# Attention chunks of 128 tokens split into two halves of 64, and the attention of a pair of chunks spread over three places between the weight products

## The chip, the cores and the metric

The kernel runs on one core of one Trainium2 chip. The metric is the device time of one execution in microseconds (us). Before the change it is 352.75 us, the median of 9 runs (352.5 to 353.03). A core has TensorE (called PE in the profile, with PEld for its weight loads), VectorE (DVE), ScalarE (ACT), GpSimd (POOL), and SyncE (SP), whose queue issues nearly all transfers here.

## The reference, cut to what matters

First comes a linear attention with decay, over 4 batches, 8 heads, 768 tokens and a head size of 48; then a feed-forward block on the 3072 tokens with d_model 384 and d_ff 1024.

```python
for t in range(S):
    cur = np.einsum('bhd,bhe->bhde', u[None] * kt, vt)
    y[:, :, t] = np.einsum('bhd,bhde->bhe', rt, state + cur)
    state = w[None, :, :, None] * state + np.einsum('bhd,bhe->bhde', kt, vt)
...
h = x @ w_in
e = np.exp(h - h_max)
solu = h * (e / (np.sum(e, axis=-1, keepdims=True) + 1e-09))
ln = (solu - mu) / np.sqrt(var + 1e-06) * g_ln
out = ln @ w_out
```

Everything is float32.

## The kernel before, in words

The tokens are cut into N = 24 chunks of T = 128 tokens, ordered so that the four batches alternate: chunk i belongs to batch i mod 4 and is its chunk number i // 4. Each batch has a state in SBUF, 128 partitions by 4 head pairs: the two heads of a pair lie in partitions 0-47 and 64-111.

The steps of one chunk, each a small function inside `direct_path`:

- `decay_k`, `decay_r`, `weigh` (L666 to L683, POOL): k and r times powers of the decay, and r·k·u per element; `sum_own` (L685, DVE) sums that per head, and `diagonal` (L689, ACT) writes it onto the diagonal of AT, the transposed score matrix, with eight instructions of 128 by 128 (L693).
- r and k are turned so that the head size lies on partitions. For the first nine chunks TensorE does it (`turn_r` L701, evicted by DVE; `turn_k` L708, evicted by ACT), from chunk 9 on a transposing DMA (`halve_rk` L872, `join_rk` L882).
- `scores` (L721): for each head pair a, half c and head q one product of 48 rows by 64 columns, with 128 moving columns for the first half of the keys and 64 for the second. `take_scores` (L732, DVE) copies them into AT under a mask, two instructions of 128 by 512.
- `heads` (L750): y, transposed, in tiles of 128 rows by 32 columns with 128 moving columns: 12 products of the state with r (not for the first chunk of a batch) and 16 of v with AT. `take_y` (L774, ACT) evicts it as xT.
- `outer` (L779): k times v in tiles of 128 by 32 with 48 moving columns; `update` (L794) adds it to the state on DVE and multiplies by the decay on POOL.
- `ffn_in` (L809): xT times w_in into h_ps, a buffer of two PSUM banks that exists once, then the exponential on ACT. `unit` (L820): a reciprocal and h times e on DVE (L826, the last reader of h_ps), then two ACT passes. `halve_ln`, `join_ln` (L861, L867): the result is turned by a transposing DMA between an ACT copy and a DVE copy. `ffn_out` (L886): the product with w_out, an ACT eviction, the store.

A float32 product appears in the trace as two matmul instructions, each with its own weight load; so a chunk's `scores` are 32 instructions, `heads` 56, `outer` 32, `ffn_in` 12 and `ffn_out` 16.

The order is written out by hand, engine by engine; each engine executes its instructions in that order. A first loop (L906, i = -2 to 6) runs one chunk per pass: from i = 2 on `ffn_in(i-2)`, the turns of chunk i+2, scores of i+1, `heads(i)`, `outer(i)`, while DVE, ACT and POOL also convert the float64 weights. The main loop (L998, i = 7, 9, ... 29) runs two chunks per pass: `ffn_in(i-2)`, `ffn_out(i-7)`, `ffn_in(i-1)`, `ffn_out(i-6)`, and then all the attention of the pair at once: scores of i+1 and i+2, `heads` of i and i+1, `outer` of both. The eight PSUM banks are two for h_ps, four fixed banks `pss` for scores and turns, and two in rotation (tag "m") for y_ps, kv_ps and o_ps.

## Time and profile before

| | |
|---|---|
| median of 9 runs | 352.75 us |
| the profiled execution's own time | 352.62 us |
| its span in the profile | 350.9 us |
| granted TensorE clock | 0.999 |
| PE busy | 334.3 us, 95%, 3427 matmuls |
| ACT, DVE, POOL busy | 240.3, 210.7, 178.8 us |
| chain that ended last, on PE | 79% |

The profile is one execution. Its time is 1.72 us longer than its span, which is the time around the recorded instructions. "PE busy" counts a matmul from its start to a modelled end, and matmuls overlap; how long a group takes is better read from the start of its first instruction to the start of the next group's first. A line such as `x32 | 26.3, 279 | 0.0` has the number of instructions, their busy time in us, the mean duration of one in ns, and the idle time before them. "128*32 128x128" is a tile of 128 rows by 32 columns of the array, with 128 rows by 128 moving columns streamed through it.

### The profile page before, as it was taken

What the parts mean: (1) busy time and instruction counts of PE and PEld (TensorE: products, weight loads), DVE (VectorE), ACT (ScalarE), POOL (GpSimd) and SP (SyncE); (2) the same over time, 40 slices, a digit from 0 to 9 for tenths busy, and PEclk for the clock granted to TensorE, in tenths of its full rate; (3) what the DMA queues carried; (4) which work ended last, traced back from release to release, by engine and by line L of the source; (5) the groups of instructions that cost most, each with busy time, mean ns of one, the idle gap of its engine ahead of it and who ended that gap; (6) DMA issues with size and microseconds to landing.
All of it is one profiled execution on the core that took longest, in us unless ns stands there. A gap on an engine that the chain in (4) does not pass through costs nothing.

```text
span 350.9 us, 8480 instructions
## 1 busy us (share of the span) xinstructions
PE 334.3 (95%) x3427; PEld 204.8 (58%) x3427; DVE 210.7 (60%) x347; ACT 240.3 (68%) x457; POOL 178.8 (51%) x196
## 2 busy tenths in 40 slices
PE   2699999999999999999999999999999999999993
PEld 2485566655664665575575575475575575555563
DVE  7795888896577568378368468469466162323420
ACT  3765988988868966866866866866867755546510
POOL 3889667789259439539539629629624000000000
PEclk9999999999999999999999999999999999999999
DMA  8999987269999999987999878865993523553541
GB/s 169 266 234 226 235 187 131 46 104 195 188 187 151 217 195 133 200 147 133 175 162 150 202 129 152 202 134 103 144 164 70 129 67 64 126 127 101 134 103 35
DMA packets 164878, 52.76 MB, mean 150 GB/s; under 512 B 157917, under 2 KB 161245, under 8 KB 164829
## 3 DMA queue, kind: packets, MB, share of 16 engines
q1 hardware_dynamic: 164684, 51.92, 78.6%
q8 instruction: 29, 0.48, 0.6%
q10 hardware_dynamic: 144, 0.20, 0.3%
q14 instruction: 21, 0.16, 0.2%
HBM read 26.94 MB, written 4.72 MB: 90 GB/s over the span
## 4 chain that ended last, share of the span: by engine, by line
PE 79%; ACT 7%; DVE 5%; issue 3%; DMA 2%; POOL 2%; POOLq 0%; DVEq 0%; ACTq 0%
PE o_ps L896 34%; PE h_ps L814 30%; PE y_ps L761 8%; PE at L728 5%; ACT AT L693 2%; ACT halves L864 2%; DVE solu L826 1%; DMA halves<-halves 1%; PE kv_ps L791 1%; DVE part L532 1%; ACT e L817 1%; DMA wq<-in_w_dram 1%; DVE AT L735 1%; ACT solu L828 1%; ACT e L829 1%
## 5 line engine op out<-in xcount | busy, mean ns | idle before, releaser
L814 PE MATMUL h_ps<-w_in_sb,xT 128*128 128x512 f32 x288 | 129.0, 597 | 1.2 <-DVE solu L826 0.7
L896 PE MATMUL o_ps<-w_out_sb,lnT 128*128 128x384 f32 (+1 forms) x400 | 127.5, 474 | 0.1
L896 PEld LDWEIGHTS o_ps<-w_out_sb,lnT 128*128 128x128 f32 x400 | 74.9, 190 | 53.1 <-issue 8.1
L814 PEld LDWEIGHTS h_ps<-w_in_sb,xT 128*128 128x128 f32 x288 | 53.5, 190 | 62.9 <-issue 57.4
L804 POOL TENSOR_TENSOR state<-state,pw 64x192 f32<-64x192 f32 x32 | 27.5, 860 | 69.2 <-DVE state L803 67.5
L693 ACT ACTIVATE AT<-ident,own 128x128 f32<-128x128 f32 x192 | 58.6, 391 | 4.9 <-DVE own L687 4.9
L864 ACT COPY halves<-solu 128x2048 uint16<-128x2048 uint16 x24 | 45.4, 1891 | 3.0 <-DMA halves<-halves 3.0
L669 POOL TENSOR_TENSOR kp<-kpad,kdec 128x512 f32<-128x512 f32 x24 | 41.5, 1729 | 6.9 <-ACT kdec L623 6.3
L828 ACT ACTIVATE solu<-solu,st 128x1024 f32<-128x1024 f32 x24 | 27.5, 1147 | 24.3 <-DVE solu L826 24.3
L817 ACT ACTIVATE e<-h_ps 128x1024 f32<-128x1024 f32 x24 | 24.5, 1019 | 25.5 <-PE h_ps L814 25.5
L735 DVE COPY_PREDICATED AT<-later,at 128x512 f32<-128x512 uint32 x48 | 31.6, 731 | 15.2 <-PE at L728 15.2
L858 DVE COPY lnT<-halves 128x2048 uint16<-128x2048 uint16 x24 | 33.6, 1419 | 6.7 <-DMA halves<-halves 6.5
L824 DVE RECIPROCAL st<-sums 128x1 f32<-128x1 f32 x24 | 3.9, 163 | 54.4 <-ACT e L817 54.2
L835 POOL TENSOR_SCALAR st<-st 128x1 f32<-128x1 f32 x24 | 7.3, 305 | 49.3 <-ACT e L829 49.2
L826 DVE SCALAR_TENSOR_TENSOR solu<-h_ps,st,e 128x1024 f32<-128x1024 f32 x24 | 30.8, 1284 | 2.1
L858 DVE COPY rk<-halves 128x2048 uint16<-128x2048 uint16 x15 | 29.3, 1953 | 0.0
L777 ACT COPY xT<-y_ps 128x384 f32<-128x384 f32 x24 | 11.5, 479 | 22.4 <-PE y_ps L761 22.4
L683 POOL TENSOR_TENSOR rku<-rku,rpad 128x384 f32<-128x384 f32 x23 | 25.7, 1115 | 1.8
L761 PE MATMUL y_ps<-AT,vt 128*32 128x128 f32 x768 | 26.3, 279 | 0.0
L898 ACT ACTIVATE o<-o_ps,st 128x384 f32<-128x384 f32 (+1 forms) x25 | 13.8, 554 | 18.1 <-PE o_ps L896 11.3
L728 PE MATMUL at<-rk 48*64 48x128 f32 (+1 forms) x768 | 26.2, 265 | 0.0
L829 ACT ACTIVATE e<-solu 128x1024 f32<-128x1024 f32 x24 | 25.4, 1057 | 0.8
(83 smaller groups left out, 346.0 us busy)
## 6 DMA issues: line engine op xcount, KB each, us to landing
raw<-in_moe_w_in_dram SPq DMA_DIRECT2D x12, 512.0 KB, 4.9
raw<-in_moe_w_out_dram SPq DMA_DIRECT2D x16, 384.0 KB, 3.9
kpad<-in_k_dram SPq DMA_DIRECT2D x24, 192.0 KB, 5.1
rpad<-in_r_dram SPq DMA_DIRECT2D x24, 192.0 KB, 5.4
vt<-in_v_dram SPq DMA_DIRECT2D x24, 192.0 KB, 5.1
out_dram<-o SPq DMA_DIRECT2D x23, 192.0 KB, 2.9
halves<-halves SPq DMA_TRANSPOSE x39, 4.9
u_bc<-in_u_dram ACTq DMA_DIRECT2D x1, 192.0 KB, 3.4
```

The source lines that it names most:

```text
L669: nc.gpsimd.tensor_mul(X["kp"].rearrange("p h d -> p (h d)"), kpads[i % NLD].rearrange("p h d -> p (h d)"), kdec.rearrange("p a d -> p (a ...
L693: nc.scalar.activation(out=AT[:, h, :], in_=ident, func=ACT.Copy, scale=X["own"][:, h])
L728: nc.tensor.matmul(ps[q][ts(c, P), a, c * P :], X["kT"][rows, a, ts(c, P)], X["rT"][rows, a, c * P :], start=True, stop=True)
L735: nc.vector.copy_predicated(A4[:, :, q, :], later.to_broadcast([128, HP, T]), live[i]["scores"][q])
L761: nc.tensor.matmul(y_ps[32 * g : 32 * g + 32, j, :], lhsT, rhs, start=(g not in opened), stop=stop, skip_group_check=True)
L814: nc.tensor.matmul(h_ps[:, ts(n, NX)], X["xT"][:, j, :], w_in_sb[:, j, ts(n, NX)], start=(j == 0), stop=(j == KD - 1))
L826: nc.vector.scalar_tensor_tensor(out=solu, in0=X["h"], scalar=rs, in1=X["e"], op0=ALU.mult, op1=ALU.mult, accum_out=tot)
L828: nc.scalar.activation(out=solu, in_=solu, func=ACT.Identity, scale=-float(dff), bias=tot)
L829: nc.scalar.activation(out=X["e"], in_=solu, func=ACT.Square, accum_out=ss)
L858: nc.vector.tensor_copy(out=words.bitcast(U16).rearrange("p n (t o) -> p o n t", o=2), in_=turned)
L864: nc.scalar.copy(out=both.rearrange("p (o n) -> p o n", o=2), in_=split(X["solu"]))
L896: nc.tensor.matmul(o_ps, X["lnT"][:, f, :], w_out_sb[:, f, part], start=(f == 0), stop=(f == KF - 1))
```

## The change

Each chunk from the third on is treated as two halves of 64 tokens, with a state between them.

- `scores` computes only the two 64 by 64 blocks on the diagonal (64 moving columns each); AT is 64 wide, `diagonal` writes 64 columns and `take_scores` moves 256 instead of 512 per head group.
- `outer` computes k times v for each half by itself, in tiles of 64 by 64, into two buffers. `middle` (new) makes the state between the halves, `mid`, from the first; `update` adds the second to `mid`. The last chunk of a batch needs only the first.
- y has two PSUM banks, one for each half. `within` (new): v times AT, each half by itself, in tiles of 64 rows by 32 columns with 64 moving columns. `carried` (new): the state times r for the first half, `mid` times r for the second, 64 moving columns each. `take_y` evicts with two instructions.
- In the main loop the work of a pair lies in three places: `attend` (scores, `outer`, `take_scores`, `middle` of the next pair) at the end of a pass, `within` after the first `ffn_in`, `carried`, `take_y` and `update` after the first `ffn_out`. The loads of k and r, POOL's decays, the turns and the diagonals are one chunk earlier; the first pass (`late`) therefore does three chunks of POOL's work and three turns instead of two.
- In the first loop `outer` and `middle` come right after `ffn_in`, both turns come before the weight conversions and `unit`, and turns and y share the two rotating banks "m". kv has two banks of its own; the scores' and, from chunk 7 on, y's banks are the same two. Chunks 0 and 1 are done as before.

```diff
+    def scores(chunks):
...
+            for a in range(HP):
+                for c in range(2):
+                    for q in range(2):
+                        nc.tensor.matmul(X["scores"][q][ts(c, U), a, :], X["kT"][rows, a, ts(c, U)],
+                                         X["rT"][rows, a, ts(c, U)], start=True, stop=True)
...
+    def within(chunks):
...
+            for n, (m, h, at) in enumerate(inner):
+                for c in range(2):
+                    nc.tensor.matmul(X["y"][c][ts(g, 32), j, :], vf[ts(c, U), at : at + 32],
+                                     AT[ts(c, U), h, :], start=(g not in opened), stop=closes,
+                                     skip_group_check=True)
...
+    def carried(i):
+        for c, St in enumerate((states[units[i][0]], X["mid"])):
+            if c == 0 and units[i][1] == 0:
+                continue
+            for m in range(12):
+                nc.tensor.matmul(X["y"][c][ts(g, 32), j, :],
+                                 St[:, a].rearrange("p q d -> p (q d)")[:, ts(n, 32)],
+                                 X["rT"][:, a, ts(c, U)], start=False, stop=True,
+                                 skip_group_check=True)
...
     def outer(chunks):
-            for a in range(HP):
-                for g in range(4):
-                    nc.tensor.matmul(X["kv"][ts(g, 32), a], X["kp"][:, h, ts(g % 2, 32)],
-                                     vt[:, h, 0:D], start=True, stop=True)
+            for a in range(HP):
+                for q in range(2):
+                    for c, dst in enumerate(X["kv"]):
+                        nc.tensor.matmul(dst[ts(q, P), a], X["kp"][ts(c, U), h, :],
+                                         vt[ts(c, U), h, 0:D], start=True, stop=True)
...
+    def middle(i):
+        for q in range(2):
+            to, kv = X["mid"][ts(q, P), :, q], X["kv"][0][ts(q, P)]
+            if c > 0:
+                nc.vector.tensor_add(to, kv, St[ts(q, P), :, q])
+            else:
+                nc.scalar.copy(out=to, in_=kv)
...
+    def attend(chunks):
+        scores(chunks)
+        outer(chunks)
+        for i in chunks:
+            take_scores(i)
+        for i in chunks:
+            middle(i)
...
+    attend([LA + LO, LA + LO + 1])
     for i in range(LA + LO, N + LA + LO, 2):
...
             ffn_in(j)
             unit(j)
+            within([i, i + 1])
...
         ffn_out(l)
+        for n in (i, i + 1):
+            if n < N:
+                carried(n)
...
         ffn_out(l + 1)
...
-        for n in now:
-            scores(n)
-        for n in now:
-            take_scores(n)
-        for n in now if i < N - 1 else []:
-            heads(n)
-            take_y(n)
-        outer(now)
+        attend([i + 2, i + 3])
```

## The prediction

> **What bounds the kernel now.** I read the page first, then PE's waits, then PE's timeline for one pass of the main loop, then the groups with shapes kept apart. The page says that TensorE is busy 95% of the span and solid from the third slice on; the two weight products alone take 129.0 and 127.5 us.

> ```profile
> PE 334.3 (95%) x3427; PEld 204.8 (58%) x3427; DVE 210.7 (60%) x347; ACT 240.3 (68%) x457; POOL 178.8 (51%) x196
> ...
> PE   2699999999999999999999999999999999999993
> ...
> L814 PE MATMUL h_ps<-w_in_sb,xT 128*128 128x512 f32 x288 | 129.0, 597 | 1.2 <-DVE solu L826 0.7
> L896 PE MATMUL o_ps<-w_out_sb,lnT 128*128 128x384 f32 (+1 forms) x400 | 127.5, 474 | 0.1
> ```

> PE's waits add to some 11 us, nearly all of them before 37 us; after that there are 0.17 us on L826 at 110.45 and 0.50 us of "issue" at 127.1. So from 36.41 us to the last o_ps, time changes by what PE has to do, and by new waits. One pass by the timeline:

> ```profile
> 174.89 1.96 PE L728 MATMUL at<-rk 48*64 48x128 f32 x64
> 176.79 0.86 PE L761 MATMUL y_ps<-rk,state 128*32 128x128 f32 x24
> 177.47 1.06 PE L761 MATMUL y_ps<-AT,vt 128*32 128x128 f32 x32
> 178.34 0.84 PE L761 MATMUL y_ps<-rk,state 128*32 128x128 f32 x24
> 179.00 1.06 PE L761 MATMUL y_ps<-AT,vt 128*32 128x128 f32 x32
> 179.87 0.86 PE L791 MATMUL kv_ps<-vt,kp 128*32 128x48 f32 x64
> 180.66 5.42 PE L814 MATMUL h_ps<-w_in_sb,xT 128*128 128x512 f32 x12
> 185.92 5.32 PE L896 MATMUL o_ps<-w_out_sb,lnT 128*128 128x384 f32 x16
> 191.08 5.31 PE L814 MATMUL h_ps<-w_in_sb,xT 128*128 128x512 f32 x12
> ```

> Starts to starts: `ffn_in` 5.16 (5.26 after kv), `ffn_out` 5.16, and the attention of the pair from 174.89 to 180.66. A pass is 180.66 - 154.08 = 26.58 us (the same line one pass earlier starts at 154.08); four undisturbed weight products are 20.62, so attention with its transitions costs **5.96 us**.

> **What one matmul costs.** The 32 of v with AT take 178.34 - 177.47 = 0.87 us. They go round four column tiles, 8 to a tile: 109 ns for 128 moving columns. kv takes 0.79 us for 64 here and 0.45 for 32 in the first loop (44.52 to 44.97); the difference, 0.34 for 32, gives 42.5 ns for 48 columns. A line through both: 0.83 ns a column plus 2.6. So 64 columns are **56 ns** in their tile. The scores agree: 16 matmuls of 128 columns follow each other in a first-half tile, 16 x 109 = 1.74 of the 1.90 us measured, and the 64-column tiles hide beside them. Sums: 1.74 + 28 x 109 ns (y) 3.05 + 16 x 42.5 ns (kv) 0.68 = 5.47; the remaining **0.49 us are transitions** between shapes. They can be placed: o to scores 0.09 (`ffn_out` from 185.92 to 191.08 takes 5.16, the one before the scores, 169.64 to 174.89, 5.25), scores to y 0.16, kv to h 0.11, h after kv 0.10, and 0.03 in y.

> ```profile
> L761 PE MATMUL y_ps<-AT,vt 128*32 128x128 f32 x768 | 26.3, 279 | 0.0
> L728 PE MATMUL at<-rk 48*64 48x128 f32 x384 | 26.2, 286 | 0.0
> L728 PE MATMUL at<-rk 48*64 48x64 f32 x384 | 21.2, 245 | 0.0
> L791 PE MATMUL kv_ps<-vt,kp 128*32 128x48 f32 x640 | 9.9, 209 | 0.5 <-issue 0.5
> ```

> **The change on PE, for a pair.**
> - Scores: still 64, all of 64 columns, over four tiles: 16 x 56 = 0.90 (before 1.74).
> - v with AT: 128 instead of 64, over eight tiles (two row halves by four columns): 16 x 56 = 0.90 (1.74). No row shows eight tiles. Bounds: 7.0 ns a matmul, if all eight run together, and 10.6 ns, the fastest pace that a group of the trace keeps (kv, 0.34/32); that end costs 0.46 more a pair. I take 7.0: kv's 10.6 is just its tile time divided by four tiles, so nothing else limits it, and the scores show that two row tiles run together.
> - State with r: 96 of 64 columns over four tiles: 24 x 56 = 1.34 (1.31).
> - kv: still 64, now 64 by 64. The weight loads bound it from above: means of 112, 139 and 190 ns (L791, L728, L896) for 32, 64 and 128 columns, about 0.8 ns a column, so 52 ns against 42.5 of streaming. Between 42.5 and 58 ns a matmul I take 52: 0.83 (0.68).
> - Transitions: three groups instead of one. Into a group 0.09, out of it 0.21, and 0.03 to 0.16 between scores and kv: 3 x 0.30 + 0.1 = about 1.0 (0.49).

> After: 0.90 + 0.90 + 1.34 + 0.83 + 1.0 = 4.97, so about **1.0 us saved a pair**. Over chunks 7 to 23: scores 17 x 0.42, v with AT 17 x 0.42, state -0.3, transitions -4.4, kv -1.0 and -0.8 for the half products that chunks 20 to 23 now need and did not have: **gain 7.8 us**.

> **The first loop, chunks 2 to 6.** There PE saves the same matmul time, but kv now stands alone behind `ffn_in` (two more transitions) and `within` and `carried` differ in shape: some 0.45 us more. For chunks 4 to 6 a pass of 9.25 us (44.97 to 54.22) becomes 8.95: 0.3 saved. Chunks 2 and 3 had no state product and now have half of one (0.34): nothing saved. Against that stand new waits. y takes the two banks that the turns just used, so `within` waits for DVE's rT (0.69 us, behind two `middle` adds of 0.35) and ACT's kT (0.57 us, behind the exponential of 1.2). For chunks 2 and 3 ACT also makes `mid`, two copies that I put at 0.33 each (L777: 0.48 for twice the columns): some 0.2 and 0.4 us lost, 0.1 for chunk 4.

> ACT is the second thing to watch; its timeline shows it late by itself in the last passes:

> ```profile
> 67.28 2.45 ACT L693 ACTIVATE AT<-ident,own 128x128 f32<-128x128 f32 x8
> 69.63 1.00 ACT L817 ACTIVATE e<-h_ps 128x1024 f32<-128x1024 f32 x1
> ...
> 78.11 2.44 ACT L693 ACTIVATE AT<-ident,own 128x128 f32<-128x128 f32 x8
> 80.46 1.00 ACT L817 ACTIVATE e<-h_ps 128x1024 f32<-128x1024 f32 x1
> ```

> `ffn_in` ended at 68.72 and its exponential began at 69.63, when the diagonals were done. This cost nothing: no one waited. Narrower diagonals save about 0.4 a chunk (306 ns start to start to some 255, by 0.75 ns a column from L898's two forms), a second y eviction gives 0.2 back, and the later rT delays L826 by some 0.6, so ACT stays as late as it was. But now (a) `within(6)` waits for kT, behind that exponential: about 1.5 us; (b) `within(8)` stands right behind `ffn_in(5)` and needs `take_scores(8)`, which needs the diagonal that ended at 80.46: about 0.9 us. What queues behind (b) on DVE is four `middle` adds, `sum_own(9)` and L826, until about 85; `ffn_in(6)` comes after `ffn_out(0)`, at about 88, so nobody waits for it. Sum for the first loop and its exit: 0.9 - 0.2 - 0.4 - 0.1 - 1.5 - 0.9 = **-2.2 us**; bounds +0.9 (every wait covered) and -4.5 (twice the waits).

> **The other engines in the main loop.** DVE loses 4 x 0.3 in `take_scores` and gains 4 x 0.36 in `middle`: nothing. `within` needs `take_scores` of the pair 7 us after the scores. `ffn_in(j)` must wait for L826 of the chunk before: `ffn_out` and attend, 7 us, against exponential, reciprocal and L826, 3 us. Cover gone, each would cost PE its full delay. POOL's decays no longer stand behind the state's multiplication of the same pair; its 16 us a pass fit into 25.6. The k and r loads go out a chunk earlier into five buffers that the decays have left; the extra POOL set, turn and join of the first pass have until attend at about 97 us, and I end them at 95. A stall there of 1 to 2 us is inside the range.

> **Sum.** 7.8 - 2.2 = 5.6 less: span 345.3, time 352.62 - 5.6 = 347.0. The profiled execution is 0.13 under the median, so this stands for the median too.

> [...]

> **Rivals.**
> 1. *Eight tiles don't all run together*, pace 10.6 ns: 17 chunks x 64 x 3.6 ns = 3.9 less gain, **350.9**. For it: no row shows eight tiles. Against: kv is explained by its tiles.
> 2. *The entry costs nothing*: ACT is early enough, gain 7.8 + 0.9 = 8.7, **343.9**. For it: shorter diagonals. Against: the exponentials of 69.63 and 80.46 are already late.
> 3. *Slower: row tiles pay a floor.* The only row-tiled group, L728, has 1.90 us for 64 = 29.7 ns a matmul. If that is a floor and not the 128-column tiles, the 256 row-tiled matmuls of a pair take 7.6 us; with 1.34 and 1.0 that is 9.9 against 5.96, +4.0 a pair, some 8 pairs: **about 385**. It decides from (5.96 - 1.34 - 1.0) / 256 = 14 ns on. Against: 16 x 109 ns explains the 1.90 without a floor.
> 4. *It does not save what it says*: transitions cost double in the new places (h to `within`, o to `carried`), 1 us more a pair: gain gone, **about 352**. Against: the four measured edges all lie at 0.09 to 0.21.

> **Chances.** Forecast 0.50 (345 to 349), rival 1 0.15, rival 2 0.15, rival 3 0.08, rival 4 0.12 (half of it slower, a third within 0.2%, the rest a little faster). 0.2% is about what a measurement of this kernel can tell from no change. From the same cases: faster 0.82, same 0.04, slower 0.14. The range takes in rivals 1 and 2 with the bounds of kv: 343.0 to 351.2.

> **What will show it.** Groups of the new profile: scores from 1.90 to about 1.05 a pair, `within` about 0.95 to 1.1, `carried` 1.4, kv 0.8 to 0.95; a pass of 25.6 us. PE's waits should show kT or DVE's `take_scores` between 60 and 83 us, 2 to 3 us in all, and none later. Wrong it would be with a new wait in every pass, or with `within` over 1.8 us a pair.

## The result, and the profile after

The changed kernel takes **362.0 us** in the median of 10 runs (355.2 to 364.6) against 352.75 (31 runs, 351.6 to 354.0): slower, ratio 1.0135, 95% interval 1.0104 to 1.0166. (The ratio leaves out runs more than 1.5% above the fastest, so it is below that of the medians; the profiled execution is such a run, and how much of its pauses the fastest, 355.2, had is not shown.) I had forecast 347.0 with 0.82 for faster: wrong, and the mechanism was in none of the rivals. The profiled execution took 360.84 us, 8.2 more than the 352.62 of before.

The page of the changed kernel, its lines in the order of those shown of before, and the instruction queue's:

```profile
PE 336.3 (94%) x4723; PEld 198.8 (55%) x4723; DVE 205.5 (57%) x387; ACT 234.7 (65%) x485; POOL 163.6 (46%) x203
...
PE   3688969997999999999999999999999999999993
...
PEclk9998998999999999999999999999999999999998
...
q8 instruction: 39, 0.64, 0.8%
...
L905 PE MATMUL h_ps<-w_in_sb,xT 128*128 128x512 f32 x288 | 133.2, 613 | 0.0
L987 PE MATMUL o_ps<-w_out_sb,lnT 128*128 128x384 f32 (+1 forms) x400 | 128.2, 476 | 0.0
```

TensorE is still the bound, but in the third, fourth, sixth and tenth slices there are holes where before had only nines from the third on, and the granted clock dips in the fourth and the seventh. The input products, the same 288 matmuls, now cost 133.2 us instead of 129.0. And the instruction queue moved 39 packets, where before had 29.

The main loop, which the prediction worked out in most detail, by TensorE's timeline (start, length):

```profile
162.40 1.16 PE L763 MATMUL at<-rk 48*64 48x64 f32 x64
163.38 1.10 PE L861 MATMUL kv_ps<-vt,kp 64*64 64x48 f32 x64
164.41 5.42 PE L905 MATMUL h_ps<-w_in_sb,xT 128*128 128x512 f32 x12
169.76 1.48 PE L822 MATMUL at<-AT,vt 64*32 64x64 f32 x128
171.17 5.43 PE L987 MATMUL o_ps<-w_out_sb,lnT 128*128 128x384 f32 x16
176.53 0.54 PE L835 MATMUL at<-rk,state 128*32 128x64 f32 x24
176.89 0.52 PE L835 MATMUL at<-rk,mid 128*32 128x64 f32 x24
177.22 0.52 PE L835 MATMUL at<-rk,state 128*32 128x64 f32 x24
177.56 0.52 PE L835 MATMUL at<-rk,mid 128*32 128x64 f32 x24
178.00 5.42 PE L905 MATMUL h_ps<-w_in_sb,xT 128*128 128x512 f32 x12
```

Start to start: scores 0.98, kv 1.03, v times AT 1.41, state times r 1.47. The same line one pass earlier starts at 138.30, so a pass is 164.41 - 138.30 = 26.11 us: 0.47 less than the 26.58 of before, not 1.0 less. From `ffn_in(7)` to the last output product it is 241.27 against 245.54 us, a **gain of 4.3**. But `ffn_in(7)` starts at 112.10 instead of 99.70: **the entry loses 12.4**, and 12.4 - 4.3 is the 8.1 us to be explained. TensorE's waits (all idle time, by line and what ended it):

```profile
PE y_ps L835 <- issue: 2.8, 1, 2.8
...
PE kv_ps L861 <- DVE state L896: 2.2, 1, 2.2
PE rd_ps L630 <- DVE state L894: 2.1, 1, 2.1
...
PE y_ps L822 <- DVE rk L724: 0.5, 1, 0.5
```

These four are 7.66 us. Two products behind them are slow; TensorE's timeline for the first of the four shows one:

```profile
48.15 0.42 PE L835 MATMUL y_ps<-rk,mid 128*32 128x64 f32 x15
51.40 0.33 PE L835 MATMUL y_ps<-rk,mid 128*32 128x64 f32 x9 [2.83 <-issue]
51.66 7.11 PE L905 MATMUL h_ps<-w_in_sb,xT 128*128 128x512 f32 x12
```

7.11 us (and 7.01 behind the pause of `rd_ps`) where 5.42 is the rule: 3.3 more. The trace's clock records show half clock for 3.41 us there. Pauses and half clock together are 11.0 of the 12.4. The other 1.4 is mostly not a loss: by `ffn_in(7)` the changed kernel has also done scores of chunk 10 and k times v of chunks 9 and 10, about 1.5 us by the times above, which before does behind `ffn_in(7)`. Counted by equal work the entry loses some 10.9 us and the main loop gains some 2.8. The passes of the first loop are longer too (62.66 to 72.19, 9.53 us, where before had 9.25), by some 1.1 us in all, about as much as the 1.2 us of waits that before has from 26 us to there (0.54, 0.48 and 0.17) and the changed kernel has not.

### The profile page after: what moved, and what is told of

Its sections match the earlier page's. It is cut to its first block, busy times and chain, and to the rows that moved or that the text cites. A ratio compares the mean times of both kernels' runs of the same rounds, so it can differ in the third digit from the quotient of the medians.

```text
span 359.1 us, 11106 instructions
## 1 busy us (share of the span) xinstructions
PE 336.3 (94%) x4723; PEld 198.8 (55%) x4723; DVE 205.5 (57%) x387; ACT 234.7 (65%) x485; POOL 163.6 (46%) x203
## 4 chain that ended last, share of the span: by engine, by line
PE 90%; DVE 3%; issue 3%; POOL 2%; ACT 0%; POOLq 0%; DVEq 0%
PE h_ps L905 37%; PE o_ps L987 35%; PE at L835 4%; PE at L822 3%; PE kv_ps L861 3%; PE at L763 3%; PE y_ps L822 1%; PE tk_ps L731 1%; PE y_ps L835 1%; PE tr_ps L723 1%; POOL kp L682 1%; PE at L746 1%; PE y_ps L794 1%; POOL vt L586 0%; DVE rk L724 0%
## 5 line engine op out<-in xcount | busy, mean ns | idle before, releaser
L905 PE MATMUL h_ps<-w_in_sb,xT 128*128 128x512 f32 x288 | 133.2, 613 | 0.0
L905 PEld LDWEIGHTS h_ps<-w_in_sb,xT 128*128 128x128 f32 x288 | 54.0, 194 | 61.6 <-issue 59.4
L897 POOL TENSOR_TENSOR state<-state,pw 64x192 f32<-64x192 f32 x36 | 18.3, 508 | 62.1 <-DVE state L896 60.3
L919 ACT ACTIVATE solu<-solu,st 128x1024 f32<-128x1024 f32 x24 | 27.5, 1147 | 27.9 <-DVE solu L917 27.7
L711 ACT ACTIVATE AT<-same,own 128x64 f32<-128x64 f32 x176 | 44.4, 338 | 1.4 <-DVE own L700 1.4
L949 DVE COPY lnT<-halves 128x2048 uint16<-128x2048 uint16 x24 | 38.9, 1637 | 5.9 <-DMA halves<-halves 5.7
L695 POOL TENSOR_TENSOR rku<-kpad,u_bc 128x384 f32<-128x384 f32 x23 | 28.3, 1230 | 15.1 <-DVE own L700 15.1
L682 POOL TENSOR_TENSOR kp<-kpad,kdec 128x512 f32<-128x512 f32 x24 | 32.0, 1334 | 5.8 <-ACT kdec L631 5.3
L949 DVE COPY rk<-halves 128x2048 uint16<-128x2048 uint16 x15 | 24.3, 1621 | 5.4 <-DMA halves<-halves 5.4
L770 DVE COPY_PREDICATED AT<-later_half,at 128x256 f32<-128x256 uint32 x44 | 16.2, 439 | 17.9 <-PE at L763 16.5
L565 DVE TENSOR_REDUCE least<-mag 128x1 f32<-128x384 f32 (+1 forms) x14 | 8.5, 607 | 28.0 <-ACT mag L563 28.0
L689 POOL TENSOR_TENSOR rp<-rpad,rdec 128x512 f32<-128x512 f32 x15 | 20.5, 1367 | 3.3 <-DVE halves L970 3.3
```

Source lines behind the costliest of these rows:

```text
L682: nc.gpsimd.tensor_mul(X["kp"].rearrange("p h d -> p (h d)"), kpads[i % NLD].rearrange("p h d -> p (h d)"), kdec.rearrange("p a d -> p (a ...
L695: engine.tensor_mul(rku, kpads[i % NLD][:, :, 0:D], u_bc)
L711: nc.scalar.activation(out=AT[:, h, :], in_=unit_matrix, func=ACT.Copy, scale=X["own"][:, h])
L905: nc.tensor.matmul(h_ps[:, ts(n, NX)], X["xT"][:, j, :], w_in_sb[:, j, ts(n, NX)], start=(j == 0), stop=(j == KD - 1))
L919: nc.scalar.activation(out=solu, in_=solu, func=ACT.Identity, scale=-float(dff), bias=tot)
L949: nc.vector.tensor_copy(out=words.bitcast(U16).rearrange("p n (t o) -> p o n t", o=2), in_=turned)
```

## The experiments

Theory A was that the whole loss is the pauses at the entry and the half clock behind them; its rival B, that the first loop is bound by ACT and DVE, or that the small tiles lose by themselves. Theory C, on the pauses' cause, and its rival D came out of the first runs.

"Pauses" are TensorE's idle stretches of 1.3 us and more after 30 us, by the profile of each kernel (the wait on `rd_ps` at 28 us is told with e1 and e2); "slow products" are input products of 6.4 us and more. The profile of e6 is of an execution of 370.9 us.

| run | median us (n) | before beside it | ratio, 95% interval | pauses, us | slow products |
|---|---|---|---|---|---|
| after | 362.03 (10) | 352.75 | 1.0135 [1.0104, 1.0166] | 2.8, 2.2 | 2 |
| e1_rd | 356.64 (4) | 353.31 | 1.0106 [1.0073, 1.0138] | 1.4, 1.9 | 1 |
| e2_upd | 361.35 (4) | 353.31 | 1.0249 [1.0206, 1.0292] | 1.8, 1.9 | 2 |
| e3_both | 357.17 (6) | 353.31 | 1.0103 [1.0063, 1.0142] | 2.2 | 1 |
| e4_oldentry | 352.81 (12) | 353.31 | 0.9972 [0.9948, 0.9997] | 2.3 | 1 |
| e5_noentry | 355.44 (6) | 352.81 | 1.0081 [1.0051, 1.0112] | 1.6, 2.9 | 1 |
| e6_onegroup | 365.33 (6) | 352.81 | 1.0345 [1.0315, 1.0374] | 1.6 and six, 12.5 in all | 5 |
| e7_cols32 | 353.32 (1) | 352.81 | a single run | 1.4, 2.9 | 1 |
| e8_pad | 356.61 (4) | 352.81 | 1.0120 [1.0093, 1.0148] | none | 0 |
| e9_spread | 355.47 (11) | 352.70 | 1.0066 [1.0045, 1.0087] | 3.4 | 1 |
| e10_shift | 362.82 (2) | 352.70 | 1.0281 [1.0256, 1.0307] | three, 7.2 in all | 2 |
| **e11_expfirst** | **349.77** (4) | 353.31 | **0.9900 [0.9883, 0.9916]** | none | 0 |

### e1 to e3: the pauses that have a named releaser

e1: the turn of `rdec` goes from chunk 1 to the start, into a bank that nobody holds.

```diff
+            turn_table(fore, rdec, psM.tile([128, HP, 128], F32, tag="kb", name="rd_ps", bufs=1))
...
-            turn_table(fore, rdec, psM.tile([128, HP, 128], F32, tag="ka", name="rd_ps", bufs=1))
```

> Of the changed kernel, only the turn of rdec is moved: from pass 1 of the first loop, where it waits for DVE to read kv's bank, to the start, behind the turn of kdec, in the other kv bank. Theory A (the change loses at the entry, by pauses of TensorE and by the half clock that follows a pause of more than 2 us): the 2.1 us pause before 28.5 us and the slow first ffn_in (7.0 instead of 5.3 us) go, the first ffn_in starts by 27.5, and the span is 3 to 4 us shorter than the changed kernel's for the same other pauses, 349 to 356. Rival B (the first loop is bound by ACT and DVE, pauses only move): the second ffn_in starts at 39 as before and the time stays within 1 us.

e2: DVE's joins and halves go behind `update(i)`, so that `outer(7, 8)` finds its banks free. e3 is both.

```diff
-        if i - LO - 1 >= 0:
-            join_ln(i - LO - 1)
-        if i + 3 >= FIRST:
-            halve_rk(i + 3)
...
             update(i)
+        if i - LO - 1 >= 0:
+            join_ln(i - LO - 1)
+        if i + 3 >= FIRST:
+            halve_rk(i + 3)
```

> Of the changed kernel, only the last pass of the first loop: join_ln(0) and halve_rk(9) stand behind update(6) instead of ahead of it, so that DVE frees kv's bank for outer(7, 8) earlier. Theory A: the 2.2 us pause of TensorE in outer(7, 8) near 83 us falls below 0.5 us and the time by about 2 us. Rival B: the wait comes back at within(8), which needs the diagonal of chunk 8 from ACT, and the gain is under 0.7 us.

> Both moves together. Theory A: about 5.5 us less than the changed kernel with the same code pause, so 350 to 353 where the pause of 2.8 us for code near 49 us stays and 346 to 348 where it goes. Rival B: within 1.5 us of the changed kernel.

e1 took the first input product from 28.94 to 27.51 and from 7.01 to 5.42 us: that wait is explained, a bank held until `update(1)` had read it. In e2 the bank was free early, but a pause stayed in k times v (TensorE's waits of e2, and its timeline there, first of after, then of e2):

```profile
PE kv_ps L861 <- issue: 1.9, 1, 1.9
PE y_ps L835 <- issue: 1.8, 1, 1.8
```

```profile
82.48 0.26 PE L861 MATMUL kv_ps<-vt,kp 64*64 64x48 f32 x2
84.92 1.14 PE L861 MATMUL kv_ps<-vt,kp 64*64 64x48 f32 x62 [2.18 <-DVE state L896]
```

```profile
80.03 0.28 PE L861 MATMUL kv_ps<-vt,kp 64*64 64x48 f32 x8
82.27 1.03 PE L861 MATMUL kv_ps<-vt,kp 64*64 64x48 f32 x56 [1.95 <-issue]
```

In after the wait was on DVE, whose last add ended at 84.86 us, and it stood behind two matmuls. In e2 it is another pause, behind eight.

"Issue" means that the profile shows nothing that the engine waits for. In after, e1 and e2 the pause in `carried(3)` stands before one and the same matmul, number 600 of the trace, nine matmuls before the end of its group (in e3 0.3 us are left of it). The 15 matmuls ahead of it in the group read the same two tiles, so a wait for data would be expected before the first of them. The times, 356.6, 361.4 and 357.2 us, all miss what theory A had forecast (349 to 356, 2 us less than after, 350 to 353): a wait that was taken away made room for another. That pauses with the half clock behind them are where the entry loses held; that a bank is the whole cause of the one in k times v did not.

### e4: the first loop of before, the main loop of after

Chunks 2 to 6 take whole scores, y and k times v again, with the banks and the order of before.

```diff
-    LA, LO, FIRST, WHOLE = 2, 5, 9, 2
+    LA, LO, FIRST, WHOLE = 2, 5, 9, 7
...
-            ffn_in(j)
-            outer([i])
-            middle(i)
+            ffn_in(j)
...
+        if units[i][1] > 0:
+            St = states[units[i][0]]
+            for m in range(12):
+                a, n = divmod(m, 3)
```

> The first loop (chunks 0 to 6) as in the kernel before, whole chunks in its order; the main loop as in the changed kernel. Theory A (all of the loss is in the first loop and its exit, the main loop gains 0.46 us a pass): the attention of a pass stays at 5.5 us, no pause over 1 us after 36 us, full clock, 347.5 to 350 us. Rival B (the smaller tiles and the new places lose by themselves): 352.5 us or more.

The first loop was as fast as before (`ffn_in` at 36.42, 44.98, 54.23, 63.48), and the main loop kept its gain. One new pause was left in between, again with a slow product behind it:

```profile
74.72 1.13 PE L763 MATMUL at<-rk 48*64 48x64 f32 x32 [2.32 <-ACT rk L733]
...
77.47 7.17 PE L919 MATMUL h_ps<-w_in_sb,xT 128*128 128x512 f32 x12
```

It took 352.8 us instead of the expected 347.5 to 350: 2.3 and 1.7 us are these two. (ACT's copy of kT ended at 74.66 us, so this wait is what its name says.) (From e4 on, lines of after stand 14 lower: L919 is its L905.)

### e5 and e6: take that wait away, then put two groups together

e5: chunk 8's copy of kT ahead of `unit`, and v times AT of the late pass behind the first output product. e6: the latter in every pass. Both have the same instructions.

```diff
+            if i == LA + LO - 1:
+                turn_k(i + 2)
             if i >= LA:
                 unit(j)
...
-            within([i, i + 1])
         decay(i + 4)
...
         ffn_out(l)
+        if late:
+            within([i, i + 1])
         for n in (i, i + 1):
             if n < N:
                 carried(n)
```

> The run before (first loop as in the kernel before, main loop of the changed kernel) came to 352.8 us, with one pause of TensorE left: scores(8) waited 2.32 us for ACT's copy of kT(8), which stood on ACT behind unit(4), and the product behind it ran at half clock (7.17 us instead of 5.4). Here that copy goes ahead of unit(4), and v times AT of chunks 7 and 8 goes from before the first output product to behind it, so that it cannot wait for the late diagonal of chunk 8. Theory A (the main loop gains what its passes show, 0.46 us each, and the whole loss is the pauses at the entry with the half clock that follows them): no pause of over 1 us after 36 us, every product at 5.2 to 5.5 us, and 2.3 + 1.7 us less: 347.5 to 349.5, faster than both kernels. Theory B (the small tiles themselves lose, pauses or not): 351 to 354, the product after the kv still at 7 us or the time given back in later passes.

> As the run with no pause at the entry, but in every pass v times AT stands next to state times r behind the first output product: two groups between the weight products instead of three. If the transitions into and out of a group are what the change pays (0.60 us in a pass for six of them, so some 0.1 to 0.2 for each pair taken away), this saves 0.15 to 0.25 us a pass, 1.2 to 2.0 us in all. Rival: the gap belongs to the shapes, not to the groups (weight loads of another tile height), then two shapes that follow each other keep it and nothing is saved (within 0.4 us).

Both went the wrong way, and that pointed at the cause. e5 has no wait for ACT, but 1.6 us of issue in k times v of chunks 7 and 8, and 2.9 in `carried`, just where v times AT now stands next to it:

```profile
PE at L845 <- issue: 2.9, 1, 2.9
...
PE kv_ps L871 <- issue: 1.6, 1, 1.6
```

e6, with the two together in every pass:

```profile
PE at L845 <- issue: 12.5, 6, 2.8
```

Two groups of small matmuls side by side, 128 and 96, cost 12.5 us in the profiled execution; with a weight product between them, in the passes of e5 behind the entry, the same matmuls had no such pause. In the passes that have no pause the merged group saves what I had expected: 25.92 us against 26.12 in e5 (151.92 to 177.84, and 145.65 to 171.77).

**What TensorE waits for is its own code, as far as these runs tell.** The instruction queue moved 0.64 MB in 39 packets in after, 16.4 KB each, and on the page of before:

```profile
q8 instruction: 29, 0.48, 0.6%
```

After has 2 x 1296 = 2592 more instructions on TensorE than before, and 10 more packets, so a packet holds some 256 instructions: 128 matmuls with their weight loads. (e5, with 2032 more, has 8 more packets, and e8, with 560 more, has 2.) In e6 the last pauses stand at matmuls 2892, 3275, 3658 and 4041 of the trace, 383 apart each time, which is three times 128 less one, while a pass has 408. They follow a grid of code blocks, not the program. All 20 issue pauses of 0.5 us and more in these profiles lie on such a grid: the matmul's number, divided by 128, leaves 73 to 88 each time, though the kernels' orders differ. The waits with a named releaser mostly do not: 917 in e4 leaves 21, 261 and 1053 in after leave 5 and 29; 1231 in after leaves 79, but stands six matmuls ahead of e2's 1237, in the same order. The trace also has the start of each packet. A few of the pauses, with what came before them:

| kernel, matmul | pause us | ends, after its packet's start | the matmul 128 earlier ran |
|---|---|---|---|
| after, 600 | 2.8 | 2.85 us | 6.2 us before the end |
| e5, 977 | 1.6 | 2.77 | 3.7 |
| e5, 1232 | 2.9 | 3.16 | 4.8 |
| e6, 3275 | 2.0 | 2.99 | 3.9 |
| e10, 2892 | 2.7 | 2.29 | 4.5 |
| before, 1487 | 0.5 | 2.89 | 3.6 |

In all 20 the end comes 2.2 to 3.2 us after a packet's start, and 128 matmuls with their pause take 3.2 to 6.2 us, 1.8 to 3.3 without it. (The waits on kT in e4 and on DVE in after end within the same ranges, so the ranges alone prove nothing; the grid, e9 and e10 carry the argument.) So a block seems to be asked for only when the one before it is in use, and to take some 3 to 6 us (my estimate, from the 3.2 to 6.2 us above): a block that is used up faster would have to wait, and a weight product in it (12 to 16 matmuls, 5.2 us) would cover that. 128 of the old small matmuls took 2.5 to 3.6 us (y and kv 1.74 + 0.79, scores and y 1.90 + 1.74), near that; the new ones take 1.4 to 2.0: the 0.50 us of issue at 127.1, which the prediction saw in the profile of before and passed over, is such a pause.

### e7 and e8: pace and padding

e7 streams only the first 32 of v times AT's 64 columns (half of the tokens get no attention within their half). e8 is the kernel before with 28 more matmul calls behind kv of chunks 2 to 6.

```diff
-                    nc.tensor.matmul(X["y"][c][ts(g, 32), j, :], vf[ts(c, U), at : at + 32],
-                                     AT[ts(c, U), h, :], start=(g not in opened), stop=closes,
+                    nc.tensor.matmul(X["y"][c][ts(g, 32), j, 0:32], vf[ts(c, U), at : at + 32],
+                                     AT[ts(c, U), h, 0:32], start=(g not in opened), stop=closes,
```

```diff
+            for n in range(28):
+                a, g = n // 4 % 4, n % 4
+                h = 2 * a + g // 2
+                nc.tensor.matmul(kv_ps[ts(g, 32), 1, a, 0:1], X["kp"][:, h, ts(g % 2, 32)],
+                                 vt[:, h, 0:1], start=True, stop=True)
```

> As the run with no pause at the entry, but v times AT streams only the first 32 of its 64 moving columns, so half of the tokens get no attention within their half. 128 matmuls as before. It took 1.27 us for 128 (9.9 ns each) where 64 columns in eight tiles at 56 ns would take 0.90. If the columns are the limit (tiles that wait for each other's streaming), the time falls toward half: 0.65 to 0.8 us. If the weight loads or their issue are the limit (one 64 by 32 load in some 10 ns), it stays at 1.1 to 1.3 us.

> The kernel before with 28 more matmul calls (56 matmuls with their weight loads, one moving column each, written to a half of the kv bank that nobody reads) behind kv of chunks 2 to 6, so that a pass of the first loop has some 196 matmuls instead of 140, as in the changed kernel. Nothing else changes. By their weight loads they cost 5 x 56 x 15 to 18 ns = 4 to 5 us. Theory code (more TensorE instructions in a pass than the instruction fetch brings in time): pauses of 1.4 to 2.8 us appear that the profile puts down to issue, where the kernel before has none over 0.5 us in these passes, and some are followed by a product of about 7 us; 357 plus 2 to 4 for each: 359 to 365. Theory data (the pauses come from the waits and the new banks, and more code alone does nothing): 356.5 to 358, no pause by issue over 0.5 us.

e7, TensorE's timeline:

```profile
163.21 1.31 PE L832 MATMUL at<-AT,vt 64*32 64x32 f32 x128
164.45 5.43 PE L1001 MATMUL o_ps<-w_out_sb,lnT 128*128 128x384 f32 x16
```

1.24 us start to start with half the columns, 1.41 with all. So the columns are not what mainly limits v times AT. The single starts show two streams in most of the group, each with a matmul every 16.6 ns, 8.3 ns a matmul, with 32 columns and with 64 alike; over the whole group, with its gaps, it is 11.0 ns for 64 (1.41 / 128). What sets the pace, the weight loads or their issue, these runs do not tell.

e8 refuted the code theory in the form that I had given it. A pass had as many matmuls as in the changed kernel, and the kernel took 3.8 us more, about what the added matmuls were expected to cost (4 to 5), with 1.0 us of issue in three short pieces (where no pause broke them, the 56 of a pass took 0.58 to 0.67 us start to start, 10 to 12 ns each, where the expectation had put an estimate of 15 to 18): 356.6, inside the rival's 356.5 to 358. So the number of instructions in a pass is not enough; what is left is how fast a block of them is used up.

### e9 and e10: two tests of the block theory

e9 adds nothing to e5 and only spreads TensorE's order at the entry: a weight product after at most some 136 small matmuls. e10 is e6 with 64 idle matmuls in front, before 7 us.

```diff
+    ffn_in(LO)
     attend([LA + LO, LA + LO + 1])
+    unit(LO)
...
+        if late:
+            ffn_in(j + 1)
         for n in (i, i + 1):
             if n < N:
                 carried(n)
...
-        if j + 1 < N:
+        if j + 1 < N and not late:
             ffn_in(j + 1)
```

```diff
+    for n in range(32):
+        nc.tensor.matmul(idle_ps[0:32], ident[:, 0:32], ident[:, 0:1], start=True, stop=True)
```

> The run with v times AT and states times r in one group of 224 had six issue pauses at states times r, 2.0 to 3.1 us each, in its passes 1, 2, 5, 6, 7 and 8 (passes 3 and 4 had none). Here 32 matmul calls (64 matmuls with weight loads, one moving column, nobody reads the result) are added in TensorE's idle time in front of 7 us. The work of the passes and its order are the same; only the place of the block borders moves, 64 matmuls earlier in every group. Theory C: a pause stands where two borders lie within one group of 224; the borders that ended the pauses lay at 189, 164, 217, 192, 167 and 142 of the group, so now they lie at 125, 100, (86 and) 153, 128, 103 and 78, with the next 128 later: passes 1, 2 and 7 lose their pause, passes 3 and 4 get one, 5 keeps one, 6 may go either way, 8 keeps one at another matmul. Theory D (these matmuls wait for something of their own, data or a bank): pauses in passes 1, 2, 5, 6, 7 and 8 again, at the same matmuls.

In e10 the pauses moved as forecast: passes 1, 2 and 7 lost theirs, 3 and 4, which had none, got one, 5 kept one, 6 lost it. Only the one forecast for pass 8 did not come. They stand at 205, 180 and 155 of the group by the timeline (77, 52 and 27 matmuls into `carried`, behind 128), where the grid of e6 gives 203, 178 and 153 (of these the forecast names the last); in e6 too the timeline has them two higher. Rival D, pauses at the same matmuls again, is ruled out. Here is the first:

```profile
142.27 0.28 PE L848 MATMUL at<-rk,mid 128*32 128x64 f32 x5
144.82 0.53 PE L848 MATMUL at<-rk,mid 128*32 128x64 f32 x19 [2.27 <-issue]
145.28 7.11 PE L922 MATMUL h_ps<-w_in_sb,xT 128*128 128x512 f32 x12
```

In e9 both issue pauses were gone and the eighth input product started at 100.50 us instead of 105.94 in e5: the 5.4 us that were expected. But the time was as in e5, 355.5 us instead of the forecast 349 to 351, since all of it was given back one pass later. TensorE's line in e9, and ACT's timeline there:

```profile
117.69 7.11 PE L919 MATMUL h_ps<-w_in_sb,xT 128*128 128x512 f32 x12 [3.37 <-DVE solu L931]
```

```profile
111.23 1.90 ACT L969 COPY halves<-solu 128x2048 uint16<-128x2048 uint16 x1 [6.24 <-DMA halves<-halves]
113.03 2.02 ACT L711 ACTIVATE AT<-same,own 128x64 f32<-128x64 f32 x8
114.95 1.00 ACT L922 ACTIVATE e<-h_ps 128x1024 f32<-128x1024 f32 x1
```

TensorE was early now, and ACT's exponential, ready since the product's end at about 105.9, stood behind a copy that waited for a DMA transpose. In e5 it ran at 113.99, only 1 us earlier, but TensorE, late by its own pauses, came to its next input product only at 119.54.

### e11: that exponential first

```diff
+        if soon:
+            ffn_in(j)
+            unit(j)
+            within([i, i + 1])
         decay(i + 4)
...
-        if j < N and not late:
+        if j < N and not late and not soon:
```

Here `soon` is the pass after the late one.

> The spread entry lost its two issue pauses (the eighth input product began at 100.50 us instead of 105.94), but gave 5.1 us back one pass later: the ninth input product waited 3.37 us for DVE's solu (117.69 instead of 114.3) and then ran at half clock (7.11 us). On ACT the exponential of the product before it (done on TensorE at 105.85) stood behind halve_ln, which waited 6.24 us for a buffer that the DMA transposes held until 111.2, and behind the diagonals: it ran at 114.95. Here, in that one pass, the input product's exponential and solu go ahead of halve_ln, the diagonals and the joins on ACT and DVE; TensorE's order is as it was. Theory C (code and the pauses it brings are the whole loss of the entry; what stays is the gain of the passes, 0.46 each): no pause over 1 us after 40 us, 355.5 - 3.4 - 1.7 = 350.4 (349 to 351.5), below both kernels. Rival (the DMA transposes are the bound at the entry: the delay only moves on to the next join): a wait of 1.5 to 3.5 us for lnT or rk in the passes behind, 353 to 356.

It took 349.77 us (349.6 to 350.1), 1.0% below the kernel before beside it and below the changed one, near the expected 350.4; its rival, that the transposes only move the delay on, stood for 353 to 356. Its first loop is still that of before, so e11 shows what the change is worth in the main loop; no run has the changed first loop without pauses. Its page:

```profile
PE 331.0 (95%) x4443; PEld 197.4 (57%) x4443; DVE 207.8 (60%) x381; ACT 234.2 (67%) x476; POOL 163.0 (47%) x199
...
PE   2698999999999999999999999999999999999992
...
PEclk9999999999999999999999999999999999999999
```

The holes and the dips of the clock are gone; from 40 us on no wait of TensorE is over 0.5 us. With them went the spread: 0.5 us over four runs, 9.5 over the ten of the changed kernel.

## Why the prediction was wrong, step by step

- **"Time changes by what PE has to do, and by new waits": right**, and the waits decided. That I listed only waits on data was the hole.
- **The first loop and its exit, -2.2: the step that failed.** It was -12.4 at `ffn_in(7)`, some -10.9 by equal work: pauses 7.7 and half clock 3.3, while longer passes (1.1) and the waits of before that went (1.2) cancel. Of the two waits I had priced, `within(6)` came at 0.5 instead of 1.5, by the profile for rT and not for kT, and `within(8)` did not come. What came was not on the list: the bank of `rd_ps` (2.1 and a slow product; e1), the code of `carried(3)` (2.8 and a slow product) and 2.2 in `outer(7, 8)` for a bank that DVE held, behind which a code pause of 1.9 stood ready when DVE was early (e2). The half clock was priced at nothing. The bound of -4.5, "twice the waits", doubled the waits I knew of, and so bounded nothing.
- **A pass of the first loop, 9.25, "becomes 8.95": wrong**, 9.53. By the timelines, start to start, scores fell from 1.02 to 0.62, but v times AT stayed (0.87, now 0.89), state times r rose from 0.68 to 1.03 (0.80 one pass earlier), kv from 0.46 to 0.61, `ffn_in` from 5.25 to 5.35 and the turns from 0.97 to 1.03.
- **"1.0 us saved a pair": the term is mis-sized, 0.47.** Scores 0.98 and state 1.47 are as worked out (1.05 and 1.4). v times AT is 1.41 where I had 0.95 to 1.1, because I took 7.0 ns a matmul from the columns, and 11.0 is what the group takes (8.3 in its steady stretches); that is **rival 1**, with its 10.6, and most of the difference. kv is 1.03 (0.8 to 0.95; the weight load that I read as 112 ns is 113 in the view, which changes nothing). Without the 2.2 that the forecast gave to the entry rival 1's time would be 348.7; e11, with the first loop of before and no pause at the entry, measures 349.8.
- **Nobody waits for `ffn_in` or ACT: right for the main loop**, where no pass of the changed kernel had a wait of 0.5 us. It holds only as long as TensorE is not early (e9).
- **Rival 3, a floor of 29.7 ns for each row tile: wrong**, 11 to 16 ns over the row-tiled groups. Rival 4, 1 us more a pair for transitions: wrong in size, since three groups cost 0.2 us more than two (e6).

What stays open: what sets the 16.6 ns of a stream, why a pause ends only 2.2 to 3.2 us after its packet's start, whether the load of the transfers beside it matters, and why one code pause forecast in e10 stayed away.

## What to carry to other kernels

On a bound engine count not only time but instructions: two profiles gave what a code packet held here (16.4 KB, some 256 instructions), and stretches of 128 matmuls that would have run in 1.8 to 3.3 us paused for up to 2.9 us without any wait for data that the profile shows. Shorter matmuls brought this kernel nearer to that (128 of the old small ones took 2.5 to 3.6 us, of the new 1.4 to 2.0), so spread the small ones between long ones rather than gathering them: gathered, those of e6 paused for 12.5 us; spread, those of e9 had no issue pause. When a pause goes, look for who was using it: in e5 the code and in e9 ACT's queue took its place at once, and only with all of them gone, and the old first loop back, did the gain of the main loop show.

## What was not expected of the hardware

- **Code supply**: within groups of small matmuls without a long one between them TensorE paused for up to 2.9 us at a time (e5), and all 20 pauses of 0.5 us and more that the profile calls "issue" lie on the grid of 128. A wait for another engine had hidden such a pause: with the 2.2 us for DVE in after gone, 1.9 of issue stood six matmuls further on in e2.
- **Half clock**: in the profiles of after and e1 to e10, of 18 pauses of 1.9 us and more ahead of an input product, 16 were followed by one of 6.4 to 7.2 us instead of 5.42 (a start every 0.85 us instead of 0.43; in after 7.11 behind the pause of 2.83, but 5.42 behind that of 2.18); of eight of 1.3 to 1.8 us only one was. So a pause of 2 to 3 us mostly cost 1.0 to 1.8 more than itself here.
